# Two linear-attention and SwiGLU layers on one core: the down projection by seven block products, Silu by its own table

## The chip, the cores and the metric

The kernel runs on one core of a Trainium2 chip. The time is that of the device in microseconds (us) for one execution of the whole program, the median of several runs. Shapes are given as partitions x elements.

## What is computed

Four layers follow each other on one sequence of S = 2048 tokens of D = 512 values in bf16. Layers 0 and 2 are a linear attention with 32 heads of 16, layers 1 and 3 a SwiGLU block with F = 1792. The weights of layers 0 and 2 are the same, and so are those of 1 and 3.

```
def attention(x, wqkv, wo):                  # x is normed; 32 heads of 16
    q, k, v = split(x @ wqkv)
    phi = lambda t: where(t > 0, t + 1, exp(t)) + 1e-6
    kv  = phi(k)^T v       per head          # 16 x 16
    z   = sum of phi(k)    over tokens
    o   = (phi(q) kv) / (phi(q) . z + 1e-6)
    return o @ wo
def ffn(x, w_gate, w_up, w_down):
    return (silu(x @ w_gate) * (x @ w_up)) @ w_down

x = x + attention(layernorm(x));  x = x + ffn(layernorm(x))
x = x + attention(layernorm(x));  x = x + ffn(layernorm(x))
```

## The kernel before

The tokens are 16 tiles of 128, in four groups of four tiles. All of x stays in SBUF as X, all weights too. The program is written as a list of operations with the buffers that they read and write; a table PROGRAM gives TensorE's order by short names, and a table ORDER gives the order on the four other queues (ACT is ScalarE, DVE is VectorE, POOL is GpSimd, SP issues DMAs). Each engine runs its list in order, and each operation waits only for what it depends on. So the two tables set everything that stands beside something else.

A name begins with the layer. `1u205` is the gate and up projection of layer 1, group 2, the sixth of the 14 tiles of F (8 matmuls of 512 columns into two PSUM banks; function `gu`). `1n6` is the down projection of token tile 6 (14 matmuls of 512 columns, one for each tile of F; function `dn`). `2k5` is the key projection of token tile 5, `2q13` a query tile of group 1, `2g5` the share of token tile 5 in K^T x, `2d13` and `2z5` the matmuls for the denominators, `0w6` the output projection of token tile 6; `k`, `q`, `g` and `w` are four matmuls of 512 columns each. `S` is a filler matmul ahead of the first data.

Around these, `ln` norms a tile: ScalarE squares it (line 496), GpSimd takes the reciprocal root (line 509), VectorE or ScalarE applies it (lines 520 and 516), and a DMA transposes it into a slot of xnT (line 529, `xT`). In layers 1 and 3 the normed tile lies in one of three buffers xnB until that DMA has landed; both the square and the apply write there. In layers 0 and 2 it lies in xnA.

`gu` needs the four transposed tiles of its group. Its SwiGLU is written with tanh, since silu(g) u = 0.5 (tanh(g/2) + 1) g u: ScalarE takes the tanh of the gate's bank into tht (line 781), VectorE forms (tanh + 1) g from tht and the bank (line 783, `gst`) and multiplies by the up bank into hT (line 786, `h`). The 0.5 is applied at the residual after the down projection (line 809, `res`), which also sums the row for the next norm. Exp, for phi, stands at line 562, its clamp at 567, and its joining at 571 or 574. All matmuls but the transposes have line 407.

PSUM has eight banks. `bank` gives out the one whose last use lies furthest back, except those that are pinned: the four accumulators of K^T x while layer 0 or 2 gathers it, and a bank of denominators.

In layers 0 and 2 the last group of queries and the output projections of a layer run beside the first tiles of the layer that follows, and so do the down projections of layer 1 beside keys and queries of layer 2.

## Time and profile before

| | |
|---|---|
| runs | 428.07, 429.51, 429.87 us; median 429.51 |
| span of the profiled execution | 427.3 us |
| TensorE busy in it | 418.4 us (98%), 2219 matmuls |
| VectorE busy | 288.3 us (67%) |
| ScalarE busy | 201.8 us (47%) |
| GpSimd busy | 82.6 us (19%) |
| matmuls of gate, up and down | 448, 448 and 462 |

The profile shows one execution. Its span runs from the first instruction to the last; the time of a run is a little above it, since starting and ending the program count too. PE is TensorE's matmuls, PEld its weight loads, which overlap them. A group of instructions is given with its line, its operands (out <- in), its count, busy time and mean length, then the idle time of its engine just before it and what ended that. Matmuls overlap each other, so the length of one (0.38 us for 512 columns) isn't what it costs; the distance between starts is.

### The profile page before, as it was taken

The numbers are of one execution on the slowest core, as the hardware profiler recorded it, in microseconds if no ns is written. First come the engines' busy times: TensorE is split into PE (matmuls) and PEld (weight loads), VectorE is DVE, ScalarE is ACT, GpSimd is POOL, SyncE is SP. The second block draws the span as 40 slices with busy tenths as digits, with TensorE's granted clock in tenths as the row PEclk, the third lists the DMA queues.
The fourth block names the chain that finished last, engine by engine and source line by source line (L and its number), as shares of the span: only waits on it lengthen the run. The fifth ranks groups of instructions, "written<-read, shape, count | busy, mean of one in ns | idle before, by whom it ended". The sixth has DMA issues, their size and how long they took to land.

```text
span 427.3 us, 6331 instructions
## 1 busy us (share of the span) xinstructions
PE 418.4 (98%) x2219; PEld 194.8 (46%) x2219; DVE 288.3 (67%) x628; ACT 201.8 (47%) x398; POOL 82.6 (19%) x206
## 2 busy tenths in 40 slices
...
GB/s 280 139 75 296 149 74 127 120 51 51 12 14 37 2 61 25 2 0 2 13 38 26 25 26 63 62 49 40 36 38 0 13 51 25 2 61 37 2 0 50
DMA packets 53279, 23.21 MB, mean 54 GB/s; under 512 B 46528, under 2 KB 52160, under 8 KB 53248
## 3 DMA queue, kind: packets, MB, share of 16 engines
...
q14 instruction: 14, 0.11, 0.1%
...
## 4 chain that ended last, share of the span: by engine, by line
PE 85%; DMA 6%; DVE 3%; ACT 2%; issue 2%; SPq 1%; POOL 1%; POOLq 0%; ACTq 0%; DVEq 0%
PE pb L407 85%; DMA xnT<-xnA 2%; DMA Wu<-in_B_w_up_dram 1%; DMA Wo<-in_A_wo_dram 1%; DMA X<-in_A_x_dram 1%; ACT etmp L562 1%; SPq L722 1%; DMA xnT<-xnB 1%; DMA RT<-rrep 1%; ACT GT L656 0%; ACT rrep L718 0%; DVE stats L486 0%; DVE xnA L520 0%; POOL rstd L509 0%; DVE X L761 0%
## 5 line engine op out<-in xcount | busy, mean ns | idle before, releaser
L781 ACT ACTIVATE tht<-pb 128x512 f32<-128x512 f32 x112 | 65.1, 594 | 128.4 <-PE pb L407 103.7
L407 PE MATMUL pb<-xnT,Wg 128*128 128x512 bf16 x448 | 115.0, 379 | 0.6 <-DMA xnT<-xnB 0.6
L407 PE MATMUL pb<-xnT,Wu 128*128 128x512 bf16 x448 | 115.0, 379 | 0.0
L783 DVE SCALAR_TENSOR_TENSOR tht<-tht,pb 128x512 f32<-128x512 f32 x112 | 75.2, 683 | 55.1 <-ACT tht L781 47.2
L407 PE MATMUL pb<-Wd,hT 128*128 128x512 bf16 (+2 forms) x462 | 99.8, 373 | 0.0
L786 DVE TENSOR_TENSOR hT<-tht,pb 128x512 bf16<-128x512 f32 x112 | 74.0, 680 | 2.9
L407 PEld LDWEIGHTS pb<-Wd,hT 128*128 128x128 bf16 x462 | 44.7, 98 | 52.4 <-DVE hT L786 0.2
L407 PEld LDWEIGHTS pb<-xnT,Wg 128*128 128x128 bf16 x448 | 43.4, 98 | 53.5 <-issue 1.5
L407 PEld LDWEIGHTS pb<-xnT,Wu 128*128 128x128 bf16 x448 | 43.6, 98 | 53.1 <-DVE hT L786 0.8
L509 POOL TENSOR_TENSOR rstd<-vpe,negh 128x1 f32<-128x1 f32 x64 | 37.5, 589 | 88.5 <-DVE vpe L505 86.6
L562 ACT ACTIVATE etmp<-pb 128x512 bf16<-128x512 f32 x64 | 36.9, 593 | 22.1 <-PE pb L407 13.8
L499 POOL TENSOR_SCALAR mv<-sums 128x1 f32<-128x1 f32 x55 | 12.5, 234 | 116.7 <-DVE X L809 61.9
L407 PE MATMUL pb<-Wqkv,xnT 128*128 128x512 bf16 x128 | 31.2, 379 | 1.9 <-DMA xnT<-xnA 0.9
L407 PE MATMUL pb<-xnT,Wqkv 128*128 128x512 bf16 x128 | 32.1, 379 | 0.0
L407 PE MATMUL pb<-pk,xnA 128*128 128x512 bf16 x128 | 31.2, 379 | 0.0
L496 ACT ACTIVATE xnB<-X,sums 128x512 bf16<-128x512 bf16 x32 | 23.0, 718 | 17.1 <-DMA xnT<-xnB 9.9
L407 PE MATMUL pb<-GT,pq 128*128 128x512 bf16 x128 | 30.2, 379 | 0.2 <-DVE pq L731 0.2
L567 DVE TENSOR_SCALAR etmp<-etmp 128x512 bf16<-128x512 bf16 x64 | 18.8, 305 | 12.7 <-ACT etmp L562 12.7
L761 DVE SCALAR_TENSOR_TENSOR X<-pb,X 128x512 bf16<-128x512 f32 x32 | 21.4, 684 | 7.2 <-PE pb L407 7.1
L809 DVE SCALAR_TENSOR_TENSOR X<-pb,X 128x512 bf16<-128x512 f32 x16 | 11.0, 688 | 19.3 <-PE pb L407 19.1
L496 ACT ACTIVATE xnA<-X,sums 128x512 bf16<-128x512 bf16 x23 | 16.5, 717 | 12.1 <-DVE X L809 11.9
L809 DVE SCALAR_TENSOR_TENSOR pq<-pb,X 128x512 bf16<-128x512 f32 (+2 forms) x17 | 10.9, 655 | 14.4 <-PE pb L407 12.3
...
## 6 DMA issues: line engine op xcount, KB each, us to landing
...
Wd<-in_B_w_down_dram POOLq DMA_DIRECT2D x3, 512.0 KB, 5.7
Wqkv<-in_A_wqkv_dram SPq DMA_DIRECT2D x2, 512.0 KB, 7.4
...
```

What stands on the lines that cost most here:

```text
L407: return op("pe", lambda e: e.matmul(o_ap, lhsT=lhsT, rhs=rhs, start=start, stop=stop, skip_group_check=skip), r=r, w=w, n=n)
L496: op("act", lambda a: a.activation(out=b_ap, in_=X[:, t, :], func=ACT.Square, scale=-float(D), bias=sums[:, t:t + 1], accum_out=mv[:, t, 1 ...
L499: op("pool", lambda p: p.tensor_scalar(out=mv[:, t, 0:1], in0=sums[:, t:t + 1], scalar1=-1.0 / D, scalar2=None, op0=ALU.mult), r=[f"sm{t}" ...
L509: op("pool", lambda p: p.tensor_tensor(out=rstd[:, t:t + 1], in0=vpe[:, t:t + 1], in1=negh[:], op=ALU.pow), r=[f"vp{t}", "negh"], w=[f"rs{ ...
L562: op("act", lambda a: a.activation(out=etmp[e][:], in_=PB[pb][:], func=ACT.Exp), r=[f"pb{pb}"], w=[f"e{e}"], kind="exp")
L567: op("dve", lambda v: v.tensor_scalar(out=etmp[e][:], in0=etmp[e][:], scalar1=1.0, scalar2=1e-6, op0=ALU.min, op1=ALU.add), r=[f"e{e}"], w ...
L722: op("sp", lambda e, tl=tl, q=q: e.dma_start(RT[R][:, :, tl * P:(tl + 1) * P], rrep[q][:], transpose=True), r=[f"rrep{q}"], w=[f"RT{R}_{tl ...
L761: op("dve", lambda v: v.scalar_tensor_tensor(out=X[:, t, :], in0=PB[pb][:], scalar=1.0, in1=X[:, t, :], op0=ALU.mult, op1=ALU.add, accum_o ...
L781: op("act", lambda e: e.activation(out=tht[a][:], in_=PB[pg][:], func=ACT.Tanh, scale=0.5), r=[f"pb{pg}"], w=[f"th{a}"], kind="tanh")
L783: op("dve", lambda v: v.scalar_tensor_tensor(out=tht[a][:], in0=tht[a][:], scalar=1.0, in1=PB[pg][:], op0=ALU.add, op1=ALU.mult), r=[f"pb{ ...
L786: op("dve", lambda v: v.tensor_tensor(out=hT[h][:, j, :], in0=tht[a][:], in1=PB[pu][:], op=ALU.mult), r=[f"pb{pu}", f"th{a}"], w=[f"h{h}_{ ...
L809: op("dve", lambda v, pb=pb, lo=lo, hi=hi: v.scalar_tensor_tensor(out=o_ap[:, lo:hi], in0=PB[pb][:, 0:hi - lo], scalar=0.5, in1=X[:, t, lo ...
```

## The change

**Down projection.** The product of a group, 512 tokens by 1792 by 512, is cut in 2 x 2 blocks: tokens in halves of 256, F in halves of 896 (seven tiles), D in halves of 256. Seven block products take the place of eight, in the form of Strassen's product with 15 sums. With A the blocks of h and B those of Wd:

- sums of h, once a group: S1 = A21 + A22, S2 = S1 - A11, S4 = A12 - S2, and A21 becomes A11 - A21. Each is written in two pieces of four and three tiles of F, so 8 instructions on VectorE (`sb` and `sa`, line 883 of the new kernel), on 128 x 1024 and 128 x 768 elements in bf16. Index 1 or 2 of A counts token halves first, then halves of F.
- sums of Wd, once for the whole kernel (`tw`): T5 = B12 - B11, T6 = B22 - T5, T4 = B21 - T6, and B12 becomes B22 - B12; 16 instructions, 12 on VectorE, 4 on GpSimd.
- products `p1` to `p7` (function `down`): two token tiles by seven tiles of F, 14 matmuls of 256 columns each, into the two halves of a bank. p1 and p2 share a bank, so do p6 and p7, and p5 and p3. The banks are pinned while a group's products run: two neighbours, and two more.
- joining: ScalarE copies p1 to f32 (`cp`), VectorE adds p6 and p7 to it (`uu`), adds X to the results (`xp`), and forms the residuals, as halves of 256 columns for two of the four token tiles (`rh`, with `tot` to add the two row sums) and as whole rows for the other two (`res`).

The sums and joins of a group lie in buffers that are free at the time (RT, pk, pq, xnA).

**Silu.** The first 20 gate tiles of layer 1 and all of layer 3 use ScalarE's Silu, and VectorE only multiplies by the up bank. The later 36 tiles of layer 1, which run beside the exps of layer 2, keep tanh and `gst`. The 0.5 moves into `h` there. The tables of ScalarE change at the first Silu of layer 1, at the first exp of layer 2, and at the first Silu of layer 3; before, one table served the whole kernel.

**Buffers.** xnB goes from 3 to 2, the slots of xnT from 6 to 4, etmp from 4 to 3, rrep from 3 to 2.

**Order.** Both tables are written anew. In the tables of `down` a name `1p06` is product 6 of group 0 in layer 1.

```diff
-3u011 3n3 3u100 2w12 3n2 3n0 3u106 3u105 2w14 3u107 3u111 3n1 3u102 3u109 3u112 3u101 3u113 3n6 3n4 3n5 3n7 3u200
...
+3u113 3u103 3u109 3u112 3p04 3p06 3u106 3u102 3p07 3u111 3u101 3p02 3p03 3u104 3u205 3u201 3p11 3p16 3p15 3u203
...
-        NXB = 3
+        xnA = sb("xnA", [P, T, D // 2], FP32)[:].bitcast(BF16)
+        NXB = 2
         xnB = [sb("xnB", [P, D], BF16) for _ in range(NXB)]
-        NXT = 6
+        NXT = 4
         xnT = [sb("xnT", [P, NC, 512], BF16) for _ in range(NXT)]
...
-        NE = 4
+        sumr = sb("sumr", [P, T], FP32)
+        NE = 3
...
-        rrep = [sb("rrep", [P, 512], BF16) for _ in range(3)]
+        rrep = [sb("rrep", [P, 512], BF16) for _ in range(2)]
...
+        NK, HT, HD = NF // 2, 2 * P, D // 2
+        Td = {i: sb("Td", [P, NK, HD], BF16) for i in (5, 6, 4)}
...
+            W11, W12, W21, W22 = (Wd[:, a:a + NK, b:b + HD] for a in (0, NK) for b in (0, HD))
+            for a, b in ((0, 2), (2, 4), (4, 6), (6, 7)):
+                js, hs = range(a, b), range(a + NK, b + NK)
+                low = [f"Wd{j}{x}" for j in js for x in "lr"]
+                for o_ap, x, y, r, w in (
+                        (Td[5], W12, W11, low, "T5"),
+                        (Td[6], W22, Td[5], [f"Wd{j}r" for j in hs] + [f"T5_{j}" for j in js], "T6"),
+                        (Td[4], W21, Td[6], [f"Wd{j}l" for j in hs] + [f"T6_{j}" for j in js], "T4"),
+                        (W12, W22, W12, [f"Wd{j}r" for j in (*js, *hs)], "Wd")):
...
+                    op("dve" if f"tw{w}{a}" in ON_ACT else "pool",
+                       lambda e, o_=o_, x_=x_, y_=y_: e.tensor_tensor(out=o_, in0=x_, in1=y_, op=ALU.subtract),
+                       r=r, w=wk, kind="tw")
...
-            op("act", lambda a: a.activation(out=etmp[e][:], in_=PB[pb][:], func=ACT.Exp),
-               r=[f"pb{pb}"], w=[f"e{e}"], kind="exp")
+            exps.append(op("act", lambda a: a.activation(out=etmp[e][:], in_=PB[pb], func=ACT.Exp),
+                           r=[f"pb{pb}"], w=[f"e{e}"], after=silus, kind="exp"))
...
-            op("act", lambda e: e.activation(out=tht[a][:], in_=PB[pg][:], func=ACT.Tanh, scale=0.5),
-               r=[f"pb{pg}"], w=[f"th{a}"], kind="tanh")
-            op("dve", lambda v: v.scalar_tensor_tensor(out=tht[a][:], in0=tht[a][:], scalar=1.0, in1=PB[pg][:],
-                                                       op0=ALU.add, op1=ALU.mult),
-               r=[f"pb{pg}", f"th{a}"], w=[f"th{a}"], kind="gst")
-            op("dve", lambda v: v.tensor_tensor(out=hT[h][:, j, :], in0=tht[a][:], in1=PB[pu][:], op=ALU.mult),
-               r=[f"pb{pu}", f"th{a}"], w=[f"h{h}_{j}"], kind="h")
+            hk = [f"h{h}_{j}a", f"h{h}_{j}b"]
+            if L == 1 and any(x > 1 for x, _ in slot_of):
+                op("act", lambda e: e.activation(out=tht[a][:], in_=PB[pg], func=ACT.Tanh, scale=0.5),
+                   r=[f"pb{pg}"], w=[f"th{a}"], kind="tanh")
+                op("dve", lambda v: v.scalar_tensor_tensor(out=tht[a][:], in0=tht[a][:], scalar=1.0, in1=PB[pg],
+                                                           op0=ALU.add, op1=ALU.mult),
+                   r=[f"pb{pg}", f"th{a}"], w=[f"th{a}"], kind="gst")
+                op("dve", lambda v: v.scalar_tensor_tensor(out=hT[h][:, j, :], in0=tht[a][:], scalar=0.5, in1=PB[pu],
+                                                           op0=ALU.mult, op1=ALU.mult),
+                   r=[f"pb{pu}", f"th{a}"], w=hk, kind="h")
+            else:
+                silus.append(op("act", lambda e: e.activation(out=tht[a][:], in_=PB[pg], func=ACT.Silu),
+                                r=[f"pb{pg}"], w=[f"th{a}"], after=exps, kind="silu"))
+                op("dve", lambda v: v.tensor_tensor(out=hT[h][:, j, :], in0=tht[a][:], in1=PB[pu], op=ALU.mult),
+                   r=[f"pb{pu}", f"th{a}"], w=hk, kind="h")
...
+            sums_of_h(L, g)
...
+        def sums_of_h(L, g):
+            before = pins.get((L, g - 1))
+            if given_u.get((L, g)) != NF or before and len(before["done"]) < NF // 2:
+                return
...
+            h = hb[L, g]
+            A11, A12, A21, A22 = (hT[h][:, a:a + NK, b:b + HT] for b in (0, HT) for a in (0, NK))
+            (S1, k1), (S2, k2), (S4, k4) = home(L, "1"), home(L, "2"), home(L, "4")
...
+            for n, (o_ap, x, y, f, r, w) in enumerate((
+                    (S1, A21, A22, ALU.add, (), k1), (S2, S1, A11, ALU.subtract, k1, k2),
+                    (S4, A12, S2, ALU.subtract, k2, k4), (A21, A11, A21, ALU.subtract, (), ()))):
+                for a, b in ((0, 4), (4, NK)):
+                    lo, hi = slice(a, b), slice(a + NK, b + NK)
+                    rk = list(r) + (kb[lo] + kb[hi], ka[lo], ka[hi], ka[lo] + kb[lo])[n]
+                    wk = list(w) or kb[lo]
+                    op("dve", lambda v, o_ap=o_ap, x=x, y=y, f=f, a=a, b=b: v.tensor_tensor(
+                        out=o_ap[:, a:b], in0=x[:, a:b], in1=y[:, a:b], op=f), r=rk, w=wk, kind="sa" if a else "sb")
...
-        def dn(L, t):
-            g, tl = divmod(t, TG)
-            h = hb[L, g]
+        FIRST = {1: 1, 2: 1, 6: 6, 7: 6, 5: 5, 3: 5, 4: 4}
+
+        def down(L, g, i):
+
+            h, d = hb[L, g], pins[L, g]
+            t0 = g * TG
+            if not d["done"]:
...
+            done = d["done"]
...
+            pb = d[FIRST[i]]
+            S = {1: hT[h][:, 0:NK, 0:HT], 2: hT[h][:, NK:, 0:HT], 4: hT[h][:, NK:, HT:], 7: hT[h][:, 0:NK, HT:]}
...
+            B = {1: Wd[:, 0:NK, 0:HD], 2: Wd[:, NK:, 0:HD], 3: Wd[:, NK:, HD:], 7: Wd[:, 0:NK, HD:], **Td}
...
+            fresh = FIRST[i] == i
+            for s in range(2):
+                for j in range(NK):
+                    kj = ks[i][j]
+                    mm(pb, S[i][:, j, s * P:(s + 1) * P], B[i][:, j, :], fresh and s == 0 and j == 0, j == NK - 1,
+                       r=(kj if isinstance(kj, list) else [kj]) + [kw[i][j]], w=[f"pb{pb}"], n=HD,
+                       cols=(s * HD, (s + 1) * HD), skip=True)
+            done.add(i)
+            (a, ka), (b, kb), (c, kc) = home(L, "a"), home(L, "b"), home(L, "c")
+            pk_ = [f"pb{pb}"]
+            av = a.rearrange("p a b -> p (a b)")
+            if i == 1:
+                op("act", lambda e: e.activation(out=av, in_=PB[pb], func=ACT.Copy), r=pk_, w=ka, kind="cp")
...
+            if i == 6:
+                op("dve", lambda v: v.tensor_tensor(out=b.rearrange("p a b -> p (a b)"), in0=PB[pb], in1=av, op=ALU.add),
+                   r=pk_ + ka, w=kb, kind="uu")
+                op("dve", lambda v: v.tensor_tensor(out=b, in0=b, in1=X[:, t0:t0 + 2, HD:], op=ALU.add),
+                   r=kb + xk[:2], w=kb, kind="xp")
+            if i == 7:
+                op("dve", lambda v: v.tensor_tensor(out=av, in0=PB[pb], in1=av, op=ALU.add),
+                   r=pk_ + ka, w=ka, kind="uu")
+            if i == 7:
+                pinned.discard(pb)
+                for s in range(2):
+                    op("dve", lambda v, s=s: v.tensor_tensor(
+                        out=c[:, 2 * s:2 * s + 2, :], in0=a[:, s, :].unsqueeze(1).to_broadcast([P, 2, HD]),
+                        in1=X[:, t0 + 2 + s, :].rearrange("p (a b) -> p a b", a=2), op=ALU.add),
+                       r=ka + [xk[2 + s]], w=kc, kind="xp")
+            if i in (2, 3):
+                for s in range(2):
+                    t = t0 + s
+                    lo = 0 if i == 2 else HD
+                    in1, rk = (X[:, t, 0:HD], [xk[s]]) if i == 2 else (b[:, s, :], kb)
+                    final(L, t, PB[pb][:, s * HD:(s + 1) * HD], in1, lo, HD, pk_ + rk, i == 2)
+                pinned.discard(pb)
+                if {2, 3} <= done:
+                    for s in range(2):
+                        ended_tile(L, t0 + s, True)
+            if {4, 5, 7} <= done and i in (4, 5, 7):
+                for s in range(2):
+                    final(L, t0 + 2 + s, two(d[4], s * HD), c[:, 2 * s:2 * s + 2, :], 0, D,
+                          [f"pb{d[4]}", f"pb{d[5]}"] + kc, True)
+                pinned.discard(d[4])
+                for s in range(2):
+                    ended_tile(L, t0 + 2 + s, False)
+            if len(done) == 7:
+                r_hT.done(h)
+                sums_of_h(L, g + 1)
+
+        ost = {}
+
...
+        def ended_tile(L, t, halves):
+
...
+            if halves:
+                op("dve", lambda v: v.tensor_tensor(out=sums[:, t:t + 1], in0=sums[:, t:t + 1], in1=sumr[:, t:t + 1],
+                                                    op=ALU.add), r=[f"sm{t}", f"sr{t}"], w=[f"sm{t}"], kind="tot")
+            ln(L + 1, t)
 
```

Where the first group of layer 1 has been through gate and up, TensorE goes on like this. Before:

```order
L407 MATMUL pb<-Wd,hT 128x512 [waits s_dve,s_act,s_qpool0]
L407 MATMUL pb<-Wd,hT 128x512 [waits s_dve]
L407 MATMUL pb<-Wd,hT 128x512 x2
L407 MATMUL pb<-Wd,hT 128x512 [waits s_qpool2]
L407 MATMUL pb<-Wd,hT 128x512 x3
L407 MATMUL pb<-Wd,hT 128x512 [waits s_qpool3]
L407 MATMUL pb<-Wd,hT 128x512 [waits s_dve]
L407 MATMUL pb<-Wd,hT 128x512 x2
L407 MATMUL pb<-Wd,hT 128x512 [waits s_qpool1]
L407 MATMUL pb<-Wd,hT 128x512
L407 MATMUL pb<-GT,pq 128x512 [waits s_dve]
L407 MATMUL pb<-GT,pq 128x512 x3
```

After, in the same place (Td are the sums of Wd, RT holds S1 and S2):

```order
L429 MATMUL pb<-Wd,hT 128x256 [waits s_dve,s_qpool1]
L429 MATMUL pb<-Wd,hT 128x256 x3
L429 MATMUL pb<-Wd,hT 128x256 [waits s_qpool0]
L429 MATMUL pb<-Wd,hT 128x256
L429 MATMUL pb<-Wd,hT 128x256 [waits s_dve]
L429 MATMUL pb<-Wd,hT 128x256 x7
L429 MATMUL pb<-Td,hT 128x256 [waits s_act]
L429 MATMUL pb<-Td,hT 128x256 x4
L429 MATMUL pb<-Td,hT 128x256 [waits s_dve]
L429 MATMUL pb<-Td,hT 128x256 x8
L429 MATMUL pb<-Td,RT 128x256 [waits s_pool,s_dve,s_act]
L429 MATMUL pb<-Td,RT 128x256 x27
```

Four products of 14 matmuls with 256 columns each stand in a row where one token tile of 14 matmuls with 512 columns stood and an output tile of layer 0 followed; the products of S1 and S2 wait for VectorE and for GpSimd.

On ScalarE, the start of layer 1: squares of its first normed tiles (into xnB and mv), the last exps of layer 0's queries (etmp, pq), and the first gate tiles (tht). Before:

```order
L496 ACTIVATE xnB,mv<-X,sums 128x512 [waits s_dve] x2
L565 ACTIVATE pq<-pb,onep 128x512 [waits s_pe]
L562 ACTIVATE etmp<-pb 128x512
L496 ACTIVATE xnB,mv<-X,sums 128x512 [waits s_dve]
L496 ACTIVATE xnB,mv<-X,sums 128x512 [waits s_qsp0,s_dve]
L562 ACTIVATE etmp<-pb 128x512 [waits s_pe]
L565 ACTIVATE pq<-pb,onep 128x512
L496 ACTIVATE xnB,mv<-X,sums 128x512 [waits s_dve,s_qsp1]
L496 ACTIVATE xnB,mv<-X,sums 128x512 [waits s_qsp2,s_dve]
L496 ACTIVATE xnB,mv<-X,sums 128x512 [waits s_qsp3,s_dve]
L781 ACTIVATE tht<-pb 128x512 [waits s_pe]
```

After:

```order
L532 ACTIVATE xnB,mv<-X,sums 128x512 [waits s_dve] x2
L603 ACTIVATE pq<-pb,onep 128x512 [waits s_pe]
L600 ACTIVATE etmp<-pb 128x512
L600 ACTIVATE etmp<-pb 128x512 [waits s_pe]
L603 ACTIVATE pq<-pb,onep 128x512
L532 ACTIVATE xnB,mv<-X,sums 128x512 [waits s_qsp0,s_dve]
L532 ACTIVATE xnB,mv<-X,sums 128x512 [waits s_qsp1,s_dve]
L532 ACTIVATE xnB,mv<-X,sums 128x512 [waits s_qsp2,s_dve]
L532 ACTIVATE xnB,mv<-X,sums 128x512 [waits s_qsp3]
L831 ACT_TABLE_LOAD [waits s_pe]
L831 ACTIVATE tht<-pb 128x512 [waits s_act]
L831 ACTIVATE tht<-pb 128x512 [waits s_pe]
```

The third square of the layer now waits for a transpose (the semaphores named qsp), where before the fourth did, two exps stand ahead of it in place of one, and a table load stands ahead of the first Silu.

On VectorE, late in layer 1, where the third group has been through gate and up (hT and tht belong to the SwiGLU; etmp and pq to the queries of layer 2). Before, with the residuals of the third group's down tiles:

```order
L786 TENSOR_TENSOR hT<-tht,pb 128x512 [waits s_pe,s_dve]
L567 TENSOR_SCALAR etmp<-etmp 128x512
L809 SCALAR_TENSOR_TENSOR X,sums<-pb,X 128x512 [waits s_pe]
L783 SCALAR_TENSOR_TENSOR tht<-tht,pb 128x512 [waits s_act,s_pe]
L786 TENSOR_TENSOR hT<-tht,pb 128x512 [waits s_dve,s_pe]
L571 TENSOR_TENSOR pq<-pq,etmp 128x512
L567 TENSOR_SCALAR etmp<-etmp 128x512
L783 SCALAR_TENSOR_TENSOR tht<-tht,pb 128x512 [waits s_pe,s_act]
L567 TENSOR_SCALAR etmp<-etmp 128x512
L809 SCALAR_TENSOR_TENSOR X,sums<-pb,X 128x512 [waits s_pe]
L786 TENSOR_TENSOR hT<-tht,pb 128x512 [waits s_dve]
L809 SCALAR_TENSOR_TENSOR X,sums<-pb,X 128x512 [waits s_pe]
```

After, with the sums of the third group:

```order
L827 SCALAR_TENSOR_TENSOR hT<-tht,pb 128x512 [waits s_pe,s_dve]
L883 TENSOR_TENSOR RT<-hT 128x1024 [waits s_dve]
L883 TENSOR_TENSOR RT<-hT 128x768 [waits s_dve]
L883 TENSOR_TENSOR hT<-hT 128x4x256
L883 TENSOR_TENSOR RT<-RT,hT 128x1024 [waits s_dve]
L824 SCALAR_TENSOR_TENSOR tht<-tht,pb 128x512 [waits s_pe,s_act]
L883 TENSOR_TENSOR RT<-RT,hT 128x768 [waits s_dve]
L827 SCALAR_TENSOR_TENSOR hT<-tht,pb 128x512 [waits s_dve,s_pe]
L824 SCALAR_TENSOR_TENSOR tht<-tht,pb 128x512 [waits s_act,s_pe]
L605 TENSOR_SCALAR etmp<-etmp 128x512
L827 SCALAR_TENSOR_TENSOR hT<-tht,pb 128x512 [waits s_dve,s_pe]
L609 TENSOR_TENSOR pq<-pq,etmp 128x512 [waits s_dve]
```

Sums of h (line 883) stand ahead of and between the two instructions of a gate tile (lines 824 and 827), where before one residual at a time stood (line 809).

## Rows read from the trace of the kernel before

**Rows 1.** The page, part 1: busy us (share of the span) x instructions.

```profile
PE 418.4 (98%) x2219; PEld 194.8 (46%) x2219; DVE 288.3 (67%) x628; ACT 201.8 (47%) x398; POOL 82.6 (19%) x206
```

**Rows 2.** TensorE's timeline in layer 3: start us, us, engine line op out<-in xcount.

```profile
299.93 1.03 PE L407 MATMUL pb<-xnT,Wg 128*128 128x512 bf16 x4
...
305.11 1.03 PE L407 MATMUL pb<-GT,pq 128*128 128x512 bf16 x4
```

**Rows 3.** Table by windows: from:to, length, busy us of each engine (instructions), clock, DMA.

```profile
62.71:100.00 37.29, 37.29 (x188) 16.96 (x187) 32.26 (x73) 19.92 (x41) 12.30 (x31) 1.00 0.41 93
115.94:234.22 118.28, 118.28 (x550) 53.58 (x549) 76.11 (x163) 58.09 (x111) 24.73 (x55) 1.00 0.11 21
240.00:280.00 40.00, 38.03 (x262) 17.90 (x261) 31.94 (x80) 22.54 (x46) 10.17 (x23) 1.00 0.24 45
```

**Rows 4.** TensorE's timeline where K^T x is multiplied by Wv.

```profile
260.54 1.06 PE L407 MATMUL pb<-GT,Wqkv 128*128 128x128 bf16 x16
```

**Rows 5.** Tile GT: loads and matmuls, duration ns min/median/max, first and last start.

```profile
L407 PEld LDWEIGHTS pb<-GT,Wqkv x32: 97/98/98, 52.1 to 261.3; 128*128 128x128 bf16 x32
L407 PE MATMUL pb<-GT,Wqkv x32: 219/219/220, 52.3 to 261.4; 128*128 128x128 bf16 x32
```

**Rows 6.** VectorE by line, 115.94 to 234.22 us: busy, mean ns, idle before, releasers.

```profile
L783 DVE SCALAR_TENSOR_TENSOR tht<-tht,pb 128x512 f32<-128x512 f32 x38 | 25.8, 684 | 17.2 <-ACT tht L781 9.4 <-PE pb L407 7.6
...
L567 DVE TENSOR_SCALAR etmp<-etmp 128x512 bf16<-128x512 bf16 x19 | 5.9, 319 | 3.3 <-ACT etmp L562 3.3
```

**Rows 7.** VectorE by line and shape, whole span.

```profile
L731 DVE TENSOR_TENSOR pq<-pq,RT 128x512 bf16<-128x512 bf16 x24 | 9.8, 413 | 4.9 <-DMA RT<-rrep 4.8
...
L626 DVE TENSOR_TENSOR GT<-GT,pk 128x512 f32<-128x512 f32 x5 | 3.5, 691 | 0.9 <-POOL GT L626 0.7
...
L809 DVE SCALAR_TENSOR_TENSOR pq<-pb,X 128x384 bf16<-128x384 f32 x1 | 0.6, 556 | 1.0 <-PE pb L407 1.0
...
L809 DVE SCALAR_TENSOR_TENSOR pq<-pb,X 128x128 bf16<-128x128 f32 x1 | 0.3, 292 | 0.2 <-PE pb L407 0.2
```

**Rows 8.** DMA issues: KB of each, median us from issue to landing.

```profile
Wd<-in_B_w_down_dram POOLq DMA_DIRECT2D x3, 512.0 KB, 5.7
...
xnT<-xnB SPq DMA_TRANSPOSE x32, 2.4
```

**Rows 9.** Timelines of GpSimd and of VectorE in layer 2.

```profile
238.52 3.81 POOL L626 TENSOR_TENSOR GT<-GT,pk 128x512 f32<-128x512 f32 x3
...
238.59 1.23 DVE L520 TENSOR_SCALAR xnA<-X,mv,rstd 128x512 bf16<-128x512 bf16 x1
```

**Rows 10.** ScalarE by line and shape.

```profile
L781 ACT ACTIVATE tht<-pb 128x512 f32<-128x512 f32 x112 | 65.1, 594 | 128.4 <-PE pb L407 103.7 <-DVE hT L786 22.5 <-DVE pk L571 1.1
...
L493 ACT ACT_TABLE_LOAD x1 | 1.3, 1283 | 1.8 <-issue 1.8
```

**Rows 11.** Timelines at the start of layer 1: ScalarE, DMA queue, TensorE.

```profile
57.60 0.72 ACT L496 ACTIVATE xnB<-X,sums 128x512 bf16<-128x512 bf16 x1 [0.18 <-DVE X L761]
...
59.14 0.72 ACT L496 ACTIVATE xnB<-X,sums 128x512 bf16<-128x512 bf16 x1 [0.73 <-DVE X L761]
...
60.06 10.72 SPq L529 DMA_TRANSPOSE xnT<-xnB  x5
...
68.07 1.02 PE L407 MATMUL pb<-xnT,Wg 128*128 128x512 bf16 x4
```

**Rows 12.** Timelines at the start of layer 3: ScalarE, TensorE.

```profile
275.03 0.72 ACT L496 ACTIVATE xnB<-X,sums 128x512 bf16<-128x512 bf16 x1 [3.30 <-DMA xnT<-xnB]
...
275.76 1.02 PE L407 MATMUL pb<-xnT,Wg 128*128 128x512 bf16 x4 [0.63 <-DMA xnT<-xnB]
```

**Rows 13.** VectorE's timeline at the head.

```profile
6.09 0.69 DVE L486 BATCH_NORM_STATS2 stats<-X 128x6 f32<-128x512 bf16 x1 [0.56 <-DMA X<-in_A_x_dram]
```

**Rows 14.** Timelines at the end: TensorE, VectorE.

```profile
419.72 4.73 PE L407 MATMUL pb<-Wd,hT 128*128 128x512 bf16 x35
...
424.49 0.29 DVE L809 SCALAR_TENSOR_TENSOR pq<-pb,X 128x128 bf16<-128x128 f32 x1 [0.23 <-PE pb L407]
```

400 lines of the change are left out of this document (233 added, 167 removed).

## The prediction

> **What bounds the kernel now.** I read the page's busy shares first: TensorE is busy for 98% of the span [rows 1]. A busy TensorE need not be one at its peak, so I went to its timeline next: between 299.93 and 305.11 us it starts six groups of four 512-wide matmuls, so a group takes 0.863 us and a matmul 215.8 ns [rows 2]. The granted clock is 1.00, the 2.4 GHz level [rows 3], at which the 512 columns alone are 213.3 ns: nothing but columns is left to save there. The table by windows says where this does not hold: from 62.71 to 100 and from 115.94 to 234.22 us TensorE has no idle time at all, from 240 to 280 it lacks 2 us of 40 [rows 3]. So the kernel is as long as its columns are, plus the head, the turn from layer 2 to layer 3, and the tail.
>
> **The down projection.** Before, a group of 512 tokens takes 4 x 14 matmuls of 512 columns; over 8 groups that is 448 (the last tile's are split in two). At 215.8 ns they are 96.7 us. After, a group takes 7 products of 2 x 7 matmuls of 256 columns, 784 in all. No row has 256 columns, so I take the two widths around it: 16 matmuls of 128 columns span 1.06 us [rows 4], of which the last is 0.22 us long, so they start 56 ns apart; their weight loads last 98 ns each and still don't slow them [rows 5]. Between 56 and 215.8 ns the line is 0.416 ns a column and 2.9 ns fixed: 109.3 ns for 256. 784 of them are 85.7 us. **Term 1: -11.0 us**, all of it on the path, since TensorE is the bound where they run. The lower bound of the cost is columns alone (106.7 ns, -13.0 us).
>
> The Trainium skill's page "TensorE: Matmul & The Clock Gate" (section Back-to-back issue gap) speaks against this: it puts a stream of weight loads and 128-column matmuls at about 81 ns a matmul, not at the bare column time. This trace has 56 ns [rows 4], and the trace decides.
>
> **What VectorE gains and loses.** Silu takes the place of tanh in 76 of the 112 tiles (20 in layer 1, all 56 in layer 3), and each drops one 512-wide VectorE instruction of 0.68 us [rows 6]: 52 us off VectorE, but off the path, as TensorE doesn't wait for it in layer 3. Against that each group gets eight sums of h. A bf16 product of two SBUF tiles of 512 takes 0.413 us; with a fixed part of 0.16 us (the line through 0.292 and 0.556 us at 128 and 384 columns) that is 0.49 ns an element [rows 7], so 0.66 us for a sum of 1024 elements and 0.54 us for 768: 4.8 us a group. Joining the products costs five 512-wide instructions (0.69 us, as the f32 sum in [rows 7]), four halves (0.42 us by the line above) and two full ones, where four full ones stood.
>
> The place to ask whether this is hidden is the second part of layer 1, where tanh stays. Before, from the 21st gate-and-up tile of layer 1 to the end of its last down tile (115.94 to 234.22 us), VectorE is busy 76.1 of 118.3 us [rows 3]. After, the same 36 tiles carry 24 sums (14.4 us), 15 wide joins (10.4), 14 halves (5.9), 8 full ones (5.5) and some small ones (1 at most), less twelve old ones (8.3): 76.1 + 28.9 = 105.0 us. TensorE has 36 x 8 + 18 x 4 wide and 22 x 14 narrow matmuls there, 77.7 + 33.7 = 111.4 us. VectorE would be at 0.91 to 0.94, the lower if the new instructions overlap their neighbours by a tenth. From 62.71 to 100 us it is busy 32.26 of 37.29 us, 0.865, and TensorE loses nothing [rows 3]. So the stretch goes a little beyond what is shown to be free, and four of the eight banks are pinned while products run. **Term 2: +1.5 us**, between 0 and rival (b).
>
> The sums of Wd are 12 instructions on VectorE (5 us) and 4 on GpSimd, in the first tiles of layer 1, where Silu has taken 20 x 0.68 us off VectorE: nothing. On GpSimd they stand ahead of the reciprocal roots of tiles 5 and 7, which the second group needs eight tiles (13.8 us) after the first; Wd takes 5.7 us to land [rows 8], four sums at the 1.27 us of the GpSimd row [rows 9] 5 us: I count nothing, and 2 us if that cover is gone. Three more table loads at 1.28 us [rows 10] fall on ScalarE, which is busy 58 of 118 us [rows 3]: nothing.
>
> **Two buffers for three.** The normed tiles of layers 1 and 3 go through xnB, now two buffers. The square of a third tile writes its buffer, so it must wait until the transpose of the first has landed. Before, the first square starts at 57.60 and its transpose at 60.06 [rows 11], and a transpose takes 2.4 us [rows 8]: 4.9 us from square to landing. With two buffers the fourth tile's landing comes no earlier than 1.5 us (57.60 to 59.14) + 4.9 + 4.9 = 11.3 us after the first square, which follows the first output tile by about 1 us (a residual and its waits). TensorE's work between that tile and the first gate tile is now, by the order, 11 output tiles, two query tiles and some small ones, 12.0 us, in layer 0 and 10.8 us in layer 2. So layer 0 misses by 0.3 us; there the first residual also stands behind a reciprocal, and the fourth tile's apply behind a query's two instructions, so up to 2.7: **term 3, +1.5 us**, where before the gate tile at 68.07 us follows the output tiles without a gap [rows 11]. In layer 2 the gap is 1.5 to 2.8 us by the same sum, where before it was 0.63; a square behind that gate waits 3.30 us for a transpose [rows 12], as the third of each group now may. **Term 4: +1.2 us** (0.6 to 2).
>
> **Head, entry, end.** The first transposed tile's copy, which comes after the statistic at 6.09 us before [rows 13], now stands behind one more of 0.69 us, and Wq is loaded ahead of four pairs of X tiles: **+0.5 us** (-1 to +1.5, as a query tile fills in early). Between the last product of layer 1 and key 12 there are 8 tiles, 6.9 us, where there were ten; the chain to it is two halves (0.84), a query's exp ahead of the square (0.6), the 4.9 from square to landing and about 1 behind others, 7.4: **+0.5 us**. The last group's second sum ends about 4.9 us after its last gate tile (0.6 for the table function as in [rows 10], 0.69 for h, then 3.4 of sums and halves), and three products of 1.53 cover 4.6: **+0.5 us** with the waits between. At the end TensorE stops at 424.45 us and a 128-wide residual starts at 424.49 [rows 14]; in its place come two halves of 0.42 us and a full output tile: **+0.9 us**.
>
> **The sum.** -11.0 + 1.5 + 1.5 + 1.2 + 0.5 + 0.5 + 0.5 + 0.9 = -4.4 us on a span of 427.3: 422.9. The median run, 429.5, lies 2.2 us above the profiled span, so I forecast 425.1 us.
>
> **Rivals.** (a) *Only columns count.* The joins hide and the order has room at every turn; then 427.3 - 11.0 + 0.9 + 2.2 = 419.4, or 420.5 with a little of each. For it: 37 us without idle time at 0.865. Against: the two-buffer chain is a dependency, which no order removes.
>
> (b) *VectorE becomes the bound in layer 1's tanh part* (slower). If VectorE keeps the 9.4 and 3.3 us that it waits there for ScalarE's tanh and exp [rows 6], 105.0 + 12.7 = 117.7 us stand against 111.4: +6.3; the first group's joins, 27.2 us by durations against 24.5 of TensorE, add 2.7. With 9.0 us in place of 1.5 the time is 432.6. It decides once VectorE is above about 0.97 there. For it: while GpSimd adds, a VectorE apply of 0.41 us takes 1.23 [rows 9], and GpSimd is busy 24.7 of 118 us [rows 3]. Against: those waits are slack, which fills first. The Trainium skill's page "SBUF — State Buffer" (section Who interferes with whom) says that a VectorE instruction with two SBUF inputs, as all the sums have, contends with a GpSimd instruction that reads SBUF; the slow apply agrees that the two engines can block each other.
>
> (c) *The turns cost their upper bounds*, and layer 1 loses 3 us: -11.0 + 3 + 2.7 + 2 + 1.5 + 1 + 0.5 + 0.9 = +0.6, so 430.1 us, no change.
>
> (d) *The loads of weights show* (slower): twice as many loads per column. Were a quarter of each 98 ns load exposed, 784 would cost 19.2 us: 444. Against it are 98 ns loads under matmuls 56 ns apart [rows 4, 5]. The Trainium skill's page on TensorE named above would give about this.
>
> **How the numbers follow.** A measurement of this kernel can tell about 0.5% from no change: below 427.4 is faster, above 431.7 slower. Forecast 0.60 (0.55 of it below 427.4), (a) 0.17, (c) 0.11, (b) 0.10, (d) 0.02. Faster 0.72, same 0.16, slower 0.12. The range 420 to 430 leaves out the lower part of (a), the upper of (c), and (b) and (d).
>
> **What would show it.** Term 1: narrow matmuls about 109 ns apart, with no gap between products. Term 2: VectorE's share in layer 1's second part at 0.9, and TensorE waits on hT or tht there of 1 to 2 us; at 0.97 with waits of 8 us (b) holds. Terms 3 and 4: a wait of the first gate tile of layers 1 and 3 on xnT, and ScalarE's third square of each waiting for a transpose; without both (a) holds. The forecast is wrong if TensorE idles in layer 3's middle, where VectorE is below 0.7, or if narrow matmuls start more than 115 ns apart.

## The result, and the profile after

The changed kernel takes 433.21 us (median of 5 runs, 431.71 to 434.53) against 429.51 before: ratio 1.0089, 95% interval 1.0063 to 1.0115. It is slower by 0.9%, where 425.1 us had been forecast and 420 to 430 given as the range. The profiled execution has a span of 431.5 us (before 427.3).

Part 1 of the page after answers to [rows 1]; of part 2, 40 equal slices in tenths, TensorE's own row and the row of its granted clock are shown.

```profile
PE 412.6 (96%) x2541; PEld 228.5 (53%) x2541; DVE 318.6 (74%) x708; ACT 210.8 (49%) x403; POOL 91.4 (21%) x205
...
PE   7999999869999999999999898899999999999996
...
PEclk9999999969999999999999999999999999999999
```

TensorE's busy time fell by 5.8 us, yet the span grew by 4.2. Two dents in TensorE's row tell where to look: the eighth and ninth slice (75.5 to 97 us), with a dent of the clock in the ninth, and the twenty-third to the twenty-sixth (237 to 280 us).

To add it up, the distance between the starts of each two neighbouring matmuls was taken, less the time of the first one's columns (215.8 ns for 512, 109.3 for 256, 56 for 128, 27 for the small ones and for the fillers at the head). What is left over is lost time, from waits or from a slow clock:

| us | before | after | e11 | e12 |
|---|---|---|---|---|
| columns of all matmuls | 413.8 | 402.7 | 402.7 | 402.7 |
| lost up to 80 us | 6.6 | 8.9 | 9.4 | 8.7 |
| lost from 80 to 124 us | 0.0 | 7.6 | 1.2 | 1.3 |
| lost in the rest of layer 1 | 0.0 | 0.0 | 0.0 | 0.0 |
| lost from the entry to layer 2 to the start of layer 3 | 2.6 | 6.0 | 5.9 | 5.0 |
| lost in layer 3 | 0.0 | 1.6 | 1.3 | 0.7 |
| ahead of the first start, behind the last | 4.4 | 4.7 | 4.7 | 4.7 |
| span | 427.3 | 431.5 | 425.3 | 423.1 |

(Rows are rounded one by one; e11 and e12 are experiments below.) The columns gave 11.1 us back, as predicted. Half of what was lost again lies at one place. TensorE's timeline there:

```profile
83.80 1.03 PE L429 MATMUL pb<-xnT,Wu 128*128 128x512 bf16 x4
89.62 1.86 PE L429 MATMUL pb<-xnT,Wg 128*128 128x512 bf16 x4 [4.80 <-DMA xnT<-xnB]
...
94.70 1.16 PE L429 MATMUL pb<-xnT,Wu 128*128 128x512 bf16 x4
95.69 1.03 PE L429 MATMUL pb<-xnT,Wg 128*128 128x512 bf16 x4
```

At 89.62 the second group of layer 1 begins. TensorE has waited 4.80 us for its transposed tiles, and then its matmuls start twice as far apart: four take 1.7 us until about 94.7, in place of 0.863. The table by windows shows the granted clock there (the last three columns are clock, DMA share, GB/s):

```profile
89.00:95.00 6.00, 5.38 (x13) 1.90 (x14) 4.92 (x15) 1.96 (x5) 1.65 (x3) 0.50 0.22 44
95.00:110.00 15.00, 15.00 (x71) 6.83 (x70) 7.29 (x17) 8.97 (x18) 2.78 (x9) 1.00 0.23 46
```

0.50 is the 1.2 GHz level, behind a stretch in which TensorE had stood idle. The wait's other end is on ScalarE: the square of the seventh tile waits for a transpose to leave its buffer.

```profile
74.90 1.52 ACT L552 ACTIVATE xnB<-X,nmr,rstd 128x512 bf16<-128x512 bf16 x2 [0.56 <-POOL nmr L549]
...
82.66 0.72 ACT L532 ACTIVATE xnB<-X,sums 128x512 bf16<-128x512 bf16 x1 [4.25 <-DMA xnT<-xnB]
```

The applies of the fifth and sixth tile end by 76.4 us, and a transpose takes 2.4 us [rows 8]. Yet the buffer comes free only at 82.6. Asked for the transposes of two short windows, the profile gives, first for the first two tiles (61 to 63.5 us), then for the fifth and sixth (75.5 to 78 us):

```profile
DMA to landing us min/median/max: 2.4/2.4/2.4
```

```profile
DMA to landing us min/median/max: 6.0/6.4/6.8
```

GpSimd issues the four loads of Wd, 1.8 MB, between 71.6 and 76.4 us; they are in flight beside those two transposes. Behind the freed buffer stand the square, the apply and the transpose of the seventh and then of the eighth tile, which lands at 89.53 us. That is when TensorE's wait ends.

### The profile page after: what moved, and what is told of

The parts are those of the page before. It is cut to its first block, busy times and chain, and to the rows that moved or that the text cites. A ratio compares the mean times of both kernels' runs of the same rounds, so it can differ in the third digit from the quotient of the medians.

```text
span 431.5 us, 7157 instructions
## 1 busy us (share of the span) xinstructions
PE 412.6 (96%) x2541; PEld 228.5 (53%) x2541; DVE 318.6 (74%) x708; ACT 210.8 (49%) x403; POOL 91.4 (21%) x205
## 4 chain that ended last, share of the span: by engine, by line
PE 79%; DVE 9%; DMA 5%; ACT 3%; issue 2%; POOL 1%; SPq 0%; ACTq 0%; DVEq 0%
PE pb L429 79%; DMA RT<-rrep 3%; DMA xnT<-xnA 2%; DVE X L799 1%; DMA xnT<-xnB 1%; DVE pq L787 1%; DVE pq L769 1%; DVE etmp L605 1%; DVE rtok L749 1%; ACT esel L455 1%; ACT rrep L756 1%; ACT etmp L600 1%; DVE xnA L556 0%; DVE pq L612 0%; DVE xnB L556 0%
## 5 line engine op out<-in xcount | busy, mean ns | idle before, releaser
L429 PE MATMUL pb<-xnT,Wg 128*128 128x512 bf16 x448 | 116.7, 383 | 7.3 <-DMA xnT<-xnB 5.9
L833 DVE TENSOR_TENSOR hT<-tht,pb 128x512 bf16<-128x512 f32 x76 | 52.0, 686 | 47.9 <-PE pb L429 34.7
L545 POOL TENSOR_TENSOR rstd<-vpe,negh 128x1 f32<-128x1 f32 x64 | 39.0, 613 | 34.4 <-DVE vpe L541 32.3
L535 POOL TENSOR_SCALAR mv<-sums 128x1 f32<-128x1 f32 x54 | 15.5, 291 | 138.5 <-DVE X L982 70.6
L429 PE MATMUL pb<-Wd,hT 128*128 128x256 bf16 x336 | 40.1, 273 | 0.0
L429 PEld LDWEIGHTS pb<-Wd,hT 128*128 128x128 bf16 x336 | 32.9, 98 | 6.6
L824 DVE SCALAR_TENSOR_TENSOR tht<-tht,pb 128x512 f32<-128x512 f32 x36 | 24.6, 683 | 3.0 <-ACT tht L822 2.7
L605 DVE TENSOR_SCALAR etmp<-etmp 128x512 bf16<-128x512 bf16 x64 | 20.7, 330 | 7.9 <-ACT etmp L600 7.3
L827 DVE SCALAR_TENSOR_TENSOR hT<-tht,pb 128x512 bf16<-128x512 f32 x36 | 24.5, 684 | 1.8
L799 DVE SCALAR_TENSOR_TENSOR X<-pb,X 128x512 bf16<-128x512 f32 x32 | 21.3, 680 | 0.0
```

The lines of the kernel that those rows point to most:

```text
L429: return op("pe", lambda e: e.matmul(o_ap, lhsT=lhsT, rhs=rhs, start=start, stop=stop, skip_group_check=skip), r=r, w=w, n=n)
L535: op("pool", lambda p: p.tensor_scalar(out=mv[:, t, 0:1], in0=sums[:, t:t + 1], scalar1=-1.0 / D, scalar2=None, op0=ALU.mult), r=[f"sm{t}" ...
L545: op("pool", lambda p: p.tensor_tensor(out=rstd[:, t:t + 1], in0=vpe[:, t:t + 1], in1=negh[:], op=ALU.pow), r=[f"vp{t}", "negh"], w=[f"rs{ ...
L605: op("dve", lambda v: v.tensor_scalar(out=etmp[e][:], in0=etmp[e][:], scalar1=1.0, scalar2=1e-6, op0=ALU.min, op1=ALU.add), r=[f"e{e}"], w ...
L799: op("dve", lambda v: v.scalar_tensor_tensor(out=X[:, t, :], in0=PB[pb], scalar=1.0, in1=X[:, t, :], op0=ALU.mult, op1=ALU.add, accum_out= ...
L824: op("dve", lambda v: v.scalar_tensor_tensor(out=tht[a][:], in0=tht[a][:], scalar=1.0, in1=PB[pg], op0=ALU.add, op1=ALU.mult), r=[f"pb{pg} ...
```

## Experiments

The baseline of each is the kernel before, run on the same chip at the same time (428.7 to 429.1 us); the ratios go by it. The experiments ran on four chips, so kernels of different groups are best compared by their ratios. In the kernels' profiles the line numbers differ by a few from after's.

**e1: the loads and sums of Wd later.**

```diff
 pool: ... 1x4.vpe -Wd.ld 1x4.pow -Wd.ld2 1x6.pow 1x4.nmr 1x6.nmr -Wd.ld3 -Wd.ld1 ... -Wd.tw -Wd.tw3
           1x5.pow 1x5.nmr 1x7.pow -Wd.tw1 -Wd.tw2 +Wd.ld +Wd.ld2 +Wd.ld3 +Wd.ld1 ... 1x10.nmr +Wd.tw +Wd.tw3 +Wd.tw1 +Wd.tw2
 dve:  twelve Wd.tw from behind 1u003.h to behind 1u008.h
```

> The changed kernel with one edit: GpSimd issues the four loads of Wd (and its four sums, and VectorE its twelve) behind the reciprocal of layer 1's eighth tile, in place of ahead of the fifth's. Theory 1 (the transfers of Wd stand beside the transposes of the fifth and sixth tile, which then land after 6.8 us in place of 2.4, and hold two buffers that the seventh and eighth square wait for): TensorE's wait of 4.8 us for the second group of layer 1 and the half clock behind it (2.6 us) go: 433.2 - 7.4 = 425.8 us. Theory 2 (two buffers in place of three are enough for that wait, whatever lies beside): the wait stays above 3 us and the time above 430. Theory 3 (GpSimd's sums of Wd ahead of the reciprocals): also gone, since they move too; it is told apart by the run with the sums on VectorE.

Measured: 443.05 us, ratio 1.0357 (1.0303 to 1.0412). The opposite of what was expected, and yet the clearest proof of the cause. The fifth and sixth tile's transposes now land after 2.4 to 2.5 us. But the loads, issued at 80.6 us, meet the next two. TensorE's wait, the piece of the chain of waits that ends it (start, us, what), and the landing of the two transposes issued from 80.5 to 83 us:

```profile
93.92 1.86 PE L427 MATMUL pb<-xnT,Wg 128*128 128x512 bf16 x4 [9.01 <-DMA xnT<-xnB]
```

```profile
82.26 11.57 DMA xnT<-xnB
```

```profile
DMA to landing us min/median/max: 7.0/9.3/11.6
```

The slow transposes moved with the loads. GpSimd's sums had moved away too, and the wait grew: they are not its cause. The Trainium skill's page "DMA: Bandwidth & Descriptors" (section Issuing engines are not separate DMA queues) says that DMAs run on the same 16 engines and interleave, whoever issues them; the traces of after and e1 agree, with 2.4 us alone against 6.0 to 11.6 beside the loads. To load Wd earlier, ahead of all these transposes, was not tried.

**e2: three buffers xnB.**

```diff
-        NXB = 2
+        NXB = 3
...
-        rT = [sb("rT", [P, TG * H], BF16) for _ in range(2)]
+        rT = [sb("rT", [P, TG * H], BF16)] * 2
...
```

> The changed kernel with three buffers xnB in place of two (rT shares one buffer for room); Wd is loaded where it was. Theory 1 (Wd's transfers): the loads and the queue on GpSimd stay, the eighth square still waits for the fifth tile's slow transpose, so the 4.8 us wait becomes 4 to 4.8 us and the half clock stays; only the waits at the first gate tile of layer 1 (1.07 us) and of layer 3 and at its second group (0.68 and 0.73 us) go: 433.2 - 2.5 = 430.7 us. Theory 2 (two buffers): the wait goes with its half clock too, 433.2 - 7.4 - 2.5 = 423.3 us.

Measured: 431.76 us, ratio 1.0071 (1.0046 to 1.0095). TensorE's wait for the second group stays, 5.1 us for 4.8 (its list of waits: us in total, times, longest):

```profile
PE pb L429 <- DMA xnT<-xnB: 6.2, 2, 5.1
```

So it isn't the step from three buffers to two that makes it. What the third buffer does give is in layer 3: 0.84 us lost at its start become 0.47, and 0.90 at its second group none. At the start of layer 1, 1.3 us stay lost (after: 1.2): there the third buffer gives nothing.

**e3: fillers in the wait.**

```diff
+            if tok == "F":
+                fb = bank()
+                for _ in range(20):
+                    mm(fb, zero[:, 0:P], zero, True, True, r=[f"h1_{NF - 1}a", f"h1_{NF - 1}b"], w=[f"pb{fb}"])
+                continue
 PROGRAM: ... 1u005 1u004 +F 1u107 1u105 ...
```

> The changed kernel with 20 matmuls of 512 columns of zeros (4.3 us) ahead of the second group's first gate tile in layer 1, where TensorE waits 4.8 us; their result is used by nothing. If the granted clock of 0.5 behind that wait comes from TensorE's idleness, the clock stays at 1.00 and the 16 matmuls behind it start 216 ns apart: 433.2 - 2.6 = 430.6 us, with the wait's end where it was, near 89.6 us. If the half clock has another cause (a heat or power limit), or what the fillers cost comes on top, the time is 433.2 or more.

Measured: 431.85 us, ratio 1.0063 (1.0048 to 1.0078), span 430.6. TensorE's timeline:

```profile
84.94 4.48 PE L428 MATMUL pb<-hT 128*128 128x512 bf16 x20
89.25 1.03 PE L428 MATMUL pb<-xnT,Wg 128*128 128x512 bf16 x4
90.12 1.03 PE L428 MATMUL pb<-xnT,Wu 128*128 128x512 bf16 x4
```

Work that is useless but there keeps the clock: the second group starts at 89.25 us (after: 89.62), and its matmuls stand at 0.87 us a four. The half clock behind the wait came from idleness. In this stretch 3.3 us are gained (7.6 lost against 4.3 of fillers); 0.7 are lost at a product near 116 us, and 2.0 at the turn to layer 3, where the clock fell to half from 266.7 to 270.1 us, for a reason that was not followed. That fall belongs to this one execution: in the other three, 0.4 to 0.7 us shorter, the mean granted clock is 1.00 over the whole span.

**e4: three buffers rrep.**

```diff
+        rrep = [rrep[0][:], rrep[1][:], hT[1][:, NF - 2, :]]
...
-        r_rrep = Ring(2)
+        r_rrep = Ring(3)
...
```

> The changed kernel with three buffers rrep in place of two (the third lies in a part of hT that is free at that time). Theory 4: at the turn from layer 2 to layer 3 the third copy waits for a transpose of 2.4 us that before did not stand in the chain; with three buffers up to 2.4 us of the 3.2 us that TensorE loses from 260 to 280 us go: 433.2 - 1.5 = 431.7 us (between 430.8 and 433.2). Rival: VectorE's row of 0.6 us instructions behind it is as late, and nothing is gained: 433.2.

Measured: 432.67 us, ratio 1.0084 (1.0067 to 1.0100). From 260 to 280 us 3.0 us are lost, after 3.2: as the rival said, nothing is gained. The buffer isn't what the turn waits for.

**e5: the first group whole, then the second.**

```diff
-1u004 1u107 1u105 1u007 1u000 1u102 1u008 0w14 1u110 1u113 0w12 1u010 0w13 1u100 1u006 1u012
+1u004 1u007 1u000 1u008 1u010 1u006 1u012 0w14 1u107 1u105 0w12 1u102 0w13 1u110 1u113 1u100
```

The same names change places in ScalarE's and VectorE's lists.

> The changed kernel with one edit of its tables: the six gate tiles of layer 1's first group that stood among those of the second group now all stand ahead of them, on every engine, so that TensorE has 14 tiles (24 us) between the first group's start and the second group's first gate tile in place of 8 (13.8 us). The loads of Wd and the two buffers stay as they are. Theory 1 (transposes slowed by the transfers of Wd, with too little work ahead of the tile that needs them; the kernel before had 12 tiles there): the eighth tile's transpose lands near 89.5 us as before, TensorE comes to it at 95 us, the wait of 4.8 us and the half clock are gone: 433.2 - 7.4 = 425.8 us. If the wait only moves to a later place (the buffers or the slots of xnT hand it on), 428 to 433.

Measured: 432.85 us, ratio 1.0075 (1.0048 to 1.0102). The second case: the wait for the second group's tiles is gone, and 30 us later there is a new one.

```profile
113.06 1.69 PE L429 MATMUL pb<-Td,hT 128*128 128x256 bf16 x14
117.80 4.88 PE L429 MATMUL pb<-Td,RT 128*128 128x256 bf16 x28 [3.05 <-DVE RT L883]
```

The product of S2 comes earlier than VectorE has S2, and the clock is at 0.50 from 118.2 to 121.6 us behind the wait. VectorE was not short of time: from 95 to 110 us it stood idle for 7 us. The sums stood in its list behind three gate tiles and a residual that were late themselves.

**e6, e7, e8: what VectorE's load costs** (all on e5's order).

```diff
 e6:
-            if L == 1 and any(x > 1 for x, _ in slot_of):
+            if True:
 e7:
-                for a, b in ((0, 4), (4, NK)):
+                for a, b in ():
 e8: the op of a sum twice, where its out is S1, S2 or S4
```

> The kernel of the run e5 with tanh and its extra VectorE instruction in all 112 gate tiles, Silu nowhere: 76 x 0.68 = 52 us more on VectorE (0.86 of layer 3 in place of 0.60, 0.92 of the first part of layer 1), three table loads fewer. As predicted (Silu takes work off VectorE where TensorE does not wait for it): within 1 us of e5, 425.8. Rival: VectorE is then late at the joins and sums of layer 3, and the time is 3 us or more above e5.

> The kernel of the run e5 without the 64 sums of h on VectorE: the products read what lies in their buffers, so the output is not the reference's. If the sums are hidden but for the last group (0.72 us wait of TensorE at 425.7 us) and the entry to layer 2 (up to 1.8 us at 243 us): 0.7 to 2.5 us below e5, about 424.3. If VectorE's sums cost in layer 1's tanh part after all: 3 us or more below.

> The kernel of the run e5 with six of the eight sums of each group computed twice, to the same place: some 3.6 us more on VectorE a group, which takes its busy share between 124 and 243 us from 0.90 (106.6 of 119 us) to 0.98. By the prediction's rival, whose point was 0.97, it begins to be the bound there: 2 to 6 us above e5 in all, of them up to 2 at the last group: about 429.5. If VectorE is far from the bound: the last group alone, 1 to 2 us above e5.

Measured: e6 446.30 us (ratio 1.0409, 1.0379 to 1.0439), e7 428.87 (1.0007, 0.9987 to 1.0028), e8 452.02 (1.0522, 1.0486 to 1.0559). The table by windows (TensorE, its loads, VectorE, ScalarE, GpSimd, clock, DMA), the rest of layer 1 in after and in e8, and layer 3 in e5 and in e6:

```profile
124.00:243.00 119.00, 119.00 (x712) 69.31 (x710) 106.57 (x233) 56.74 (x109) 22.39 (x50) 1.00 0.08 16
```

```profile
124.00:252.00 128.00, 119.81 (x714) 69.55 (x713) 114.33 (x243) 54.19 (x102) 20.78 (x45) 0.99 0.07 13
```

```profile
283.00:428.00 145.00, 143.33 (x856) 83.50 (x856) 87.39 (x155) 50.67 (x93) 13.14 (x31) 1.00 0.12 28
```

```profile
295.00:441.00 146.00, 143.89 (x855) 82.91 (x855) 124.50 (x212) 50.07 (x92) 13.04 (x32) 1.00 0.11 28
```

With VectorE at 106.57 of 119 us (0.90) TensorE loses nothing; with 18 sums more in the same work (some 11 us by their durations, an estimate) TensorE stands idle for 8.2 of 128. So there is a bound above the change's load. Where it begins no run shows: nothing was tried between 0.90 and about 0.99 of these 119 us, and in e8 VectorE is itself busy for only 114.33 of the 128 us, so the lists' order costs before the engine is full. In all, e8 lies 19 us above e5, where 2 to 6 had been expected.

In layer 3, 37 us more on VectorE (0.60 to 0.85) cost about 1 us. That agrees with the prediction; but e6 lies 13.4 us above e5, where 1 at most or 3 and more had been expected, the latter in layer 3. It loses 8.6 us more than e5 from 60 to 140 us, where the sums of Wd and h, the residuals and the gate tiles stand together, and 4.2 at the turn to layer 3, where its clock fell to half (not followed). I read the 8.6 us so: without Silu the sums have no room in the first part of layer 1. This is not shown: some of it may be the order's, which was written for Silu, and from 84 to 119 us VectorE is busy for 27.8 of 35 us there.

e7 lies 4.0 us below e5, and the 4.2 us that e5 loses from 100 to 120 us are gone in its profile (taken in a run 1.2 us below the median): beyond that wait the sums of h cost next to nothing.

**e9, e11: where the sums stand.** VectorE's list from the first group's last product h on (only sums, h and residuals):

```diff
 e5:  1u012.h 0w14.res 1u107.h 1u105.h 0w12.res 1u102.h 0w13.res sb sb3 1u110.h 1u113.h 1u100.h sa 0w15.res sb1 sa3 sa1 sb2 sa2
 e9:  1u012.h sb sb3 sa sb1 sa3 sa1 sb2 sa2 0w14.res 1u107.h 1u105.h 0w12.res 1u102.h 0w13.res 1u110.h 1u113.h 1u100.h 0w15.res
 e11: 1u012.h 0w14.res sb 1u107.h sa 1u105.h 0w12.res sb1 1u102.h 0w13.res sa1 sb3 1u110.h sa3 1u113.h sb2 1u100.h 0w15.res sa2
```

> The kernel of the run e5 with the first group's eight sums of h moved up VectorE's list, right behind the last product h of that group (12 us ahead of the first product on TensorE), in place of behind three gate tiles of the second group and four output tiles' residuals. Theory: the 3.2 us wait that e5 had before the product of S2 (114.5 us), and the half clock from 118.2 to 121.6 us behind it (1.7 us), come only from the sums' place in the list: 432.85 - 4.9 = 428.0 us. Rival: the sums wait for something that is as late (the tables' other entries, the sums of Wd), and the time stays above 431.

> The kernel of the run e5 with the first group's eight sums of h neither behind the second group's tiles (e5: TensorE waited 3.2 us for them) nor in one block ahead of them (e9: a residual and a bank waited 4.4 us behind the block), but one by one between those tiles' products and residuals, into the 7 us in which VectorE stood idle there from 95 to 110 us. Theory: the two waits have no other cause than the place in VectorE's list, both go, and the half clock with them: 432.85 - 4.9 = 428.0 us. Rival: that stretch has no room on any list, and some wait of 3 us or more stays: 431 or more.

Measured: e9 432.83 us (1.0102, 1.0082 to 1.0121), e11 427.39 (0.9968, 0.9957 to 0.9980). In e9 the block of sums fills VectorE from 101.8 to 106.6 us, and TensorE waits for the residual behind it:

```profile
107.30 1.89 PE L428 MATMUL pb<-GT,pq 128*128 128x512 bf16 x4 [4.28 <-DVE X L798]
```

In e11 both waits are gone, and the clock stays at 1.00. Against after, e5 and e11 move names in lists and nothing else, and win 5.8 us (5.2 by the ratios); e11 even lies below e7, which has no sums at all.

**e10, e12: with four edits more.**

```diff
 e2's three buffers
-twWd4 twWd6
+twT50 twT60 twWd0 twWd2 twWd4 twWd6          (all sums of Wd on VectorE)
 act: ... 2M1.evac 2M0.evac +2M2.evac          dve: -2M2.evac
 dve: ... 1p33.tot +2x12.tot 2x14.apply 2x15.apply 2q21.ts -2x12.tot ...
```

> e9 with four more edits: three buffers xnB; GpSimd's four sums of Wd on VectorE (beside them an apply and a product of VectorE took 1.24 and 1.37 us in place of 0.41); one of two evacuations of the turn from layer 2 to layer 3 from VectorE to ScalarE; the sum of two row sums of tile 12 (layer 2) moved up VectorE's list, ahead of two applies and a query's clamp. If the waits are what the trace names: 2.5 us for the buffers, 1.2 for GpSimd, 0.6 and 1.2 for the two moves, 428.0 - 5.5 = 422.5 us, below the kernel before (429). Rival: the waits are handed on to the next engine as in e5, and the time is 426 or more.

> e11 with the four edits of e10 (three xnB, all sums of Wd on VectorE, one evacuation to ScalarE, tile 12's sum of row sums moved up). Without the wait of 3.9 us that e10 kept near 104 us, and its half clock (1.7 us): 430.7 - 5.6 = 425.1 us, 0.9% below the kernel before. If the waits of this stretch are handed on once more: 429 or more.

Measured: e10 (on e9) 430.71 us (1.0040, 1.0026 to 1.0055), with 3.9 us lost at e9's place; e12 (on e11) 424.78 us (0.9913, 0.9897 to 0.9930), faster than both kernels. Part 1 of e12's page and the clock's row:

```profile
PE 409.3 (97%) x2541; PEld 227.2 (54%) x2541; DVE 316.3 (75%) x711; ACT 210.5 (50%) x404; POOL 86.8 (21%) x201
...
PEclk9999999999999999999999999999999999999999
```

Of the four, the buffers gave 0.9 us in layer 3 (0.83 and 0.58 lost in e11, 0.47 and none in e12). The move of `tot` gave 0.86 at the entry to layer 2 (1.31 lost became 0.45), but 0.64 were lost anew at 247 us. The evacuation gave 0.48 at the turn to layer 3, in e10 (against e9) as in e12 (against e11); e2's three buffers alone give nothing there. The sums of Wd on VectorE gave nothing (1.3 us lost from 80 to 124 us, in e11 1.2). The rest of the 2.1 us between the spans, 0.7, lies ahead of 80 us, where profiles of one and the same head differ by more than that (see the small terms below).

## Why the prediction was wrong

**The step that failed** is the one on the sums of Wd: "I count nothing, and 2 us if that cover is gone". It asked whether GpSimd's sums would be done before the second group's reciprocals, and set Wd's 5.7 us to land against the cover of eight gate tiles. It did not ask what lands beside Wd. By the new order four tiles of the second group are still to be transposed then; before, the second group began with the thirteenth gate tile, and one transpose stood there, landing after 4.2 us (the median in [rows 8] hides it). Price: 4.8 us of wait, 2.6 us of half clock behind it, and 0.2 around them. With these 7.6 us the forecast span of 422.9 becomes 430.5, against 431.5 (from span to median it is 1.7 us in after, for the 2.2 that the forecast added). No rival named this, and the one that lies nearest to the time, (b) with 432.6, is wrong: its mechanism doesn't show.

**Term 1** was right: columns fell from 413.8 to 402.7 us, -11.1 for -11.0, and the narrow matmuls start 109.3 ns apart (14 of them from 116.41 to 117.94). The line's fixed part comes out as 2.7 ns and not 2.9, which changes nothing.

```profile
116.41 1.69 PE L429 MATMUL pb<-Wd,hT 128*128 128x256 bf16 x14
117.94 1.69 PE L429 MATMUL pb<-Td,hT 128*128 128x256 bf16 x14
```

Their weight loads don't show; rival (d) is out, and the longer gap of the Trainium skill's page "TensorE: Matmul & The Clock Gate" (section Back-to-back issue gap), which the prediction named beside it, isn't seen at this width either.

**Term 2** (+1.5) is 0.0: VectorE's share is 0.90, a little under the forecast's 0.91 to 0.94, and TensorE never waits from 124 to 243 us. A sum takes 0.69 and 0.55 us (0.66 and 0.54 estimated). That rival (b) decides above 0.97 was not measured; e8, at about 0.99, shows a loss. "52 us off VectorE, but off the path" holds for layer 3 (e6); for the first part of layer 1 e6 points the other way, to sums that need what Silu frees, without showing it.

**Term 3** (+1.5) has nearly its size, 1.2 us at the first gate tile of layer 1, but the buffers are not its cause: three of them leave it (e2, e12). In e2 the fourth square waits 0.17 us for a buffer and starts at 65.06, but the fourth apply comes at 68.50, behind residuals and a query's joining in VectorE's list. This is the other part of the chain that the term named. **Term 4** (+1.2) is 0.84 us at the start of layer 3 (before 0.80) and 0.90 at its second group, 0.9 more than before. There the buffers are the cause, as forecast: e2 takes away 1.3 of the 1.7. Yet e3 and e7, with two buffers, lose nothing at the second group either; they come to layer 3 after 1.6 to 2.0 us more lost at the turn.

**The small ones.** Entry to layer 2: 1.8 us for 0.5; e12 shows that half of it was a sum of two numbers standing behind a clamp that waits for an exp, though most of what its move gave was lost again.

The last group: 0.7 us for 0.5, and that is luck. The forecast put it on the group's second sum of h, but e7, which has no sums, waits as long at the same place (after, then e7):

```profile
426.57 1.70 PE L429 MATMUL pb<-Wd,pk 128*128 128x256 bf16 x14 [0.56 <-DVE pq L982]
```

```profile
421.09 1.70 PE L423 MATMUL pb<-Wd,pk 128*128 128x256 bf16 x14 [0.56 <-DVE pq L976]
```

The last product, p3, goes into the bank of p5, and waits for the two whole-row residuals that read it (lines 982 and 976).

End: 0.4 for 0.9 (from the last start on, 3.5 us for 3.1). Head, up to 40 us: 0.3 for 0.5, which one profile can't tell: the matmul that after starts at 40.09 us starts between 40.16 and 41.62 us in the profiles of e2, e4, e5, e7 and e9 to e12, whose head is the same.

Not in the sum at all: some 0.9 us more from 40 us to the first gate tile of layer 1, and 1.6 between the entry to layer 2 and layer 3 (2.7 more at the turn itself, less 1.1 that before lost at 247 us). e4 excludes the buffers rrep. With one evacuation less on VectorE e10 and e12 lose 0.48 us less there, so VectorE's row of products and evacuations makes a part of the turn's loss; the cause of the rest stays open.
